# Attention backward on one core: three passes over the scores replaced by one loop of small TensorE tiles

## The chip, the cores and the metric

The kernel runs on one core of a Trainium2 chip. The metric is the device time in microseconds (us) of one execution. In the listings PE is TensorE (the matmul engine), PEld its weight loads, DVE is VectorE, ACT is ScalarE, POOL is GpSimd and SP the Sync engine, whose queue issues most DMAs (transfers). SBUF is the working memory of the core; matmuls write their results to PSUM, which VectorE and ScalarE read. The granted clock is the share of TensorE's full clock that the profile records; it stands at 1 or at 0.5 here. A tile of TensorE is a part of its 128 x 128 array: 32*128 in a listing means 32 rows and 128 columns.

## The reference

The program is the forward and the whole backward of two attention blocks, A and B, on separate inputs. Their outputs stand side by side. Block A is a linear attention and the change does not touch its arithmetic. Block B is softmax attention with 16 heads of width 28 and one shared K and V:

```python
def _B_ref(x, wq, wk, wv, wo):           # x 1x2048x448, H = 16, Dh = 28
    q = (x @ wq).reshape(B, S, H, Dh) ...                 # per head
    k = x @ wk                                            # shared by all heads
    v = x @ wv
    scores = einsum("bhqd,bkd->bhqk", q, k) * (Dh ** -0.5)
    p = softmax(scores)
    o = einsum("bhqk,bkd->bhqd", p, v)
    return o.reshape(B, S, H * Dh) @ wo
# result: out = concat(A, B) and the gradients of all eight inputs, for a given grad_out, in bf16
```

In the backward, with e = exp(scale * score) and do = grad_out_B @ wo^T, the costly products per head, query and key are these: score, dp = do.v, o = sum e*v, ds = e * (dp - D), dq = sum ds*k, dk = sum ds*q, dv = sum e*do. D is a row sum of do*o. There are 16 x 2048 x 2048 scores, which is 1024 tiles of 128 x 512. The contraction or the result of every product is only 28 wide. Both kernels pad it to 32.

## The kernel before

Block B walks over all scores three times. All matmuls use the whole array. Since a head is only 32 rows wide, four heads are put into one 128-row operand, and the other operand is block-expanded: 4 blocks of 32 rows on the diagonal and zeros elsewhere.

```python
# 1. forward: e goes to the o product and to DRAM
for g in range(4):                       # four heads each
    for qp in range(QPAIRS):             # 256 queries
        block_expand(qblk, ...)
        for t in range(NS):              # 128 keys
            st_ps = psS.tile([P, 1024], F32, name="st_ps")
            for hv in range(2):
                mm(st_ps[:, hv * 512:(hv + 1) * 512], kT_rep[:, t * P:(t + 1) * P], qblk[:, hv, :])
            e = ework.tile([P, 1024], BF16, name="e")
            nc.scalar.activation(out=e[:], in_=st_ps[:, :], func=ACT.Exp, scale=scale)
            for hv in range(2):
                mm(oaccs[hv][:, :], vaug_rep4[:, t, :], e[:, hv * 512:(hv + 1) * 512], ...)
            eng.dma_start(edram[r0:r0 + P, :], e[:, :])
# ... o, D, and don = do / rowsum, with D folded in as one more column ...
# 2. dv and dk: scores again, this time with queries on the partitions
for t in range(NS):
    for qt in range(NS):
        for g in range(4):
            mm(s_ps[:, :], qT_B[g][:, qt * P:(qt + 1) * P], kblk[:, t, :])
            nc.scalar.activation(out=e[:], in_=s_ps[:, :], func=ACT.Exp, scale=scale)
            mm(dp_ps[:, :], doT2_B[g][:, qt * P:(qt + 1) * P], vblk[:, t, :])
            nc.vector.tensor_tensor(out=ds_sb[:, :], in0=dp_ps[:, :], in1=e[:, :], op=ALU.mult)
            mm(dvT_acc[:, :], don2_B[:, qt, g * P:(g + 1) * P], e[:, :], ...)
            mm(dkT_acc[:, :], qn_B[:, qt, g * P:(g + 1) * P], ds_sb[:, :], ...)
# 3. dq: e back from DRAM, with keys on the partitions
for g in range(4):
    for qb in range(NS):
        for t in range(NS):
            # every second t: DMA of e from edram
            mm(dpt_ps[:, :], vT_rep[:, t * P:(t + 1) * P], dblk[:, qb, :])
            # dsT = dpt_ps * e on VectorE (every third by way of a ScalarE copy)
            mm(dqacc[:, :], kn_rep4[:, t, :], dsT[:, :], start=(t == 0), stop=(t == NS - 1))
# ... weight gradients, output of B ...
```

## Time and profile before

| what | value |
|---|---|
| median time, 4 runs | 2837.94 us (2831.61 to 2847.09) |
| profiled span | 2839.7 us |
| block A | 0 to 393 us |
| projections of B | 393 to 530 us |
| pass 1, forward | 530 to 1096 us (566 us, 1.10 us per exp of 1024 columns) |
| middle | 1096 to 1205 us |
| pass 2, dv and dk | 1205 to 2180 us (975 us, 0.95 us per tile) |
| pass 3, dq | 2180 to 2786 us (606 us, 0.59 us per tile) |
| tail | 54 us |

The page of the kernel before gives, in parts 1 and 4, the busy time of TensorE and the chain of work that ended last, by engine:

```profile
PE 2506.8 (88%) x11290; PEld 1063.8 (37%) x11290; DVE 1709.6 (60%) x3498; ACT 1516.5 (53%) x2431; POOL 210.7 (7%) x310
...
PE 70%; ACT 15%; DVE 7%; issue 4%; DMA 2%; POOL 1%; SPq 0%; ACTq 0%; POOLq 0%; DVEq 0%
```

An average over the span hides that each stage has its own limit. The view by stretches of the kernel before shows it. Its columns are the stretch, its length, the busy us of each engine with the number of instructions, the granted TensorE clock, the busy share of the DMA engines, and GB/s:

```profile
core 0: us, PE busy (x) PEld busy (x) DVE busy (x) ACT busy (x) POOL busy (x), PEclk, DMA share, GB/s
...
530.00:1096.00 566.00, 501.39 (x2047) 197.65 (x2047) 111.91 (x398) 500.30 (x514) 138.33 (x255) 0.99 0.65 239
1096.00:1205.00 109.00, 81.39 (x407) 39.14 (x407) 90.84 (x389) 12.22 (x23) 7.47 (x2) 0.86 0.08 26
1205.00:2180.00 975.00, 972.36 (x4348) 419.76 (x4346) 714.13 (x1072) 586.20 (x1037) 0.05 (x1) 1.00 0.01 2
2180.00:2786.00 606.00, 503.09 (x2076) 200.40 (x2077) 546.82 (x1044) 260.32 (x579) 27.65 (x4) 0.97 0.71 221
```

In the second pass TensorE is busy 972 of 975 us: that pass is bound by matmuls. In the forward pass ScalarE is busy 500 of 566 us, and it does one exp of 1023 ns after another. The costliest groups of the kernel before (part 5 of the page: line, engine, operation, tiles and shapes, count; then busy us and mean ns of one; then the idle time just before them and what ended it) say what is done twice:

```profile
L780 DVE TENSOR_TENSOR ds_sb<-dp_ps,e 128x512 bf16<-128x512 f32 x1024 | 689.2, 692 | 250.8 <-PE s_ps L96 137.2 <-PE dp_ps L96 85.5 <-ACT e L776 24.8
L776 ACT ACTIVATE e<-s_ps 128x512 bf16<-128x512 f32 x1024 | 583.6, 596 | 403.7 <-DVE ds_sb L780 292.9 <-PE s_ps L96 84.6
L650 ACT ACTIVATE e<-st_ps 128x1024 bf16<-128x1024 f32 x512 | 498.8, 1023 | 64.5 <-PE st_ps L96 62.5 <-ACT e L650 2.0
```

The exps of pass 2 (583.6 us busy) repeat those of pass 1 in the other layout. The three passes take 2256 us from 530 to 2786, with the middle part among them.

One more reading matters, since the change uses the array in several tile modes. The time line of the kernel before has a place where a 128-row matmul is followed by one of 64 rows:

```profile
441.59 0.38 PE L96 MATMUL projN_ps<-wqB_pad,xb_T_3270 128*128 128x512 bf16 x1
441.90 0.39 PE L96 MATMUL projN_ps<-wqB_pad,xb_T_3271 64*128 64x512 bf16 x1
442.22 0.23 PE L96 MATMUL ps_vn<-wvB_rep,xb_T_3268 128*128 128x128 bf16 x1
```

The starts are 0.31 and 0.32 us apart, where two 128-row matmuls of that size are 0.22 apart. A change of mode costs about 0.1 us here.

### The profile page before, as it was taken

To read this page: it belongs to the slowest core of one execution; us is meant where nothing else is said; L and a number is where in the kernel's file an instruction comes from. 1 tells how busy PE (TensorE), PEld (TensorE's weight loads), DVE (VectorE), ACT (ScalarE), POOL (GpSimd) and SP (SyncE) were. 2 spreads that over 40 slices of the span, in tenths; PEclk is the share of its full clock that TensorE was granted. 3 is DMA by queue.
4 is the path that set the end of the run, shared out by engine and by line. 5 is a ranking of instruction groups with operands and counts; after the bars stand their busy time and mean duration, and the time that the engine had idled before them with its cause. 6 is when DMAs were issued, how large, how long until landed. Compare 5 with 4: busy or idle time off the path is not lost.

```text
span 2839.7 us, 35260 instructions
## 1 busy us (share of the span) xinstructions
PE 2506.8 (88%) x11290; PEld 1063.8 (37%) x11290; DVE 1709.6 (60%) x3498; ACT 1516.5 (53%) x2431; POOL 210.7 (7%) x310
## 2 busy tenths in 40 slices
PE   4777988788888888799999999999998878888788
PEld 1334533233333333344444444444443333333333
DVE  4758402122222225777777777777776989989892
ACT  1220124888888884156666566666564444444342
POOL 1000002122222221000000000000000000000000
PEclk9887988799999999799999999999999999999999
DMA  6020210466666663000000000000001767767672
GB/s 71 1 77 4 46 59 1 156 238 241 240 239 241 238 240 116 28 1 1 1 1 1 1 1 1 1 1 1 1 1 46 239 212 233 239 207 239 206 240 71
DMA packets 266987, 296.65 MB, mean 104 GB/s; under 512 B 66464, under 2 KB 217536, under 8 KB 266800
## 3 DMA queue, kind: packets, MB, share of 16 engines
q1 hardware_dynamic: 246016, 226.82, 25.9%
q0 software_dynamic: 20784, 67.58, 6.5%
q8 instruction: 88, 1.44, 0.2%
q14 instruction: 99, 0.81, 0.1%
HBM read 144.02 MB, written 144.02 MB: 101 GB/s over the span
## 4 chain that ended last, share of the span: by engine, by line
PE 70%; ACT 15%; DVE 7%; issue 4%; DMA 2%; POOL 1%; SPq 0%; ACTq 0%; POOLq 0%; DVEq 0%
PE dkT_acc L96 10%; ACT e L650 9%; PE dp_ps L96 9%; PE dpt_ps L96 8%; PE s_ps L96 8%; PE dvT_acc L96 8%; PE dqacc L96 7%; PE st_ps L96 4%; PE tps_set L100 2%; PE gw_acc L96 1%; ACT dpt_sb L826 1%; PE ps_gx L96 1%; PE projT_ps L96 1%; PE ps_gxB L96 1%; POOL dblkT L808 1%
## 5 line engine op out<-in xcount | busy, mean ns | idle before, releaser
L780 DVE TENSOR_TENSOR ds_sb<-dp_ps,e 128x512 bf16<-128x512 f32 x1024 | 689.2, 692 | 250.8 <-PE s_ps L96 137.2
L776 ACT ACTIVATE e<-s_ps 128x512 bf16<-128x512 f32 x1024 | 583.6, 596 | 403.7 <-DVE ds_sb L780 292.9
L650 ACT ACTIVATE e<-st_ps 128x1024 bf16<-128x1024 f32 x512 | 498.8, 1023 | 64.5 <-PE st_ps L96 62.5
L96 PE MATMUL dpt_ps<-dblkT,vT_rep 128*128 128x512 bf16 x1024 | 388.9, 383 | 100.6 <-ACT dpt_sb L826 57.0
L96 PE MATMUL dkT_acc<-ds_sb,qn_B 128*128 128x512 bf16 x1024 | 385.8, 377 | 2.0 <-DVE ds_sb L780 1.8
L96 PE MATMUL dvT_acc<-e,don_B 128*128 128x512 bf16 x1024 | 385.1, 378 | 0.3 <-ACT e L776 0.3
L96 PE MATMUL dqacc<-dsT,kn_rep_3252 128*128 128x512 bf16 x1024 | 379.7, 381 | 2.1 <-DVE dsT L829 1.5
L826 ACT ACTIVATE dpt_sb<-dpt_ps 128x512 bf16<-128x512 f32 x320 | 191.1, 597 | 293.3 <-PE dpt_ps L96 291.3
L96 PE MATMUL st_ps<-qblk,kT_rep 128*128 128x512 bf16 x1024 | 305.8, 380 | 9.2 <-ACT qT_B_3247 L613 9.2
L642 DVE MEMSET qblk<- 128x512 uint32 x32 | 15.5, 485 | 462.5 <-PE st_ps L96 412.6
L96 PEld LDWEIGHTS <-vaug_rep_3250 128*128 128x128 bf16 x1024 | 99.2, 97 | 244.7 <-issue 184.4
L96 PEld LDWEIGHTS <-kn_rep_3252 128*128 128x128 bf16 x1024 | 99.8, 97 | 240.9 <-issue 157.9
L656 POOL DMA_DIRECT2D edram<-e x256 | 138.9, 542 | 484.9 <-ACT e L650 484.7
L96 PEld LDWEIGHTS <-vT_rep 128*128 128x128 bf16 x1024 | 99.7, 98 | 163.7 <-DVE dblkT L224 27.0
L96 PEld LDWEIGHTS <-don_B 128*128 128x128 bf16 x1024 | 98.5, 96 | 136.0 <-issue 43.9
L96 PEld LDWEIGHTS <-kT_rep 128*128 128x128 bf16 x1024 | 98.7, 96 | 134.1 <-issue 13.1
L96 PEld LDWEIGHTS <-qn_B 128*128 128x128 bf16 x1024 | 99.3, 97 | 122.6 <-issue 1.6
L808 POOL MEMSET dblkT<- 128x8192 bf16 x4 | 27.7, 6925 | 1421.5 <-PE dp_ps L96 989.9
L96 PE MATMUL s_ps<-kblk,qT_B_3244 128*128 128x512 bf16 x256 | 97.2, 380 | 8.0 <-DVE kblk L224 8.0
L96 PE MATMUL dp_ps<-vblk,doT_B_9380 128*128 128x512 bf16 x256 | 97.0, 379 | 0.3 <-DVE vblk L224 0.3
L96 PE MATMUL s_ps<-kblk,qT_B_3245 128*128 128x512 bf16 x256 | 97.3, 380 | 0.0
L96 PE MATMUL dp_ps<-vblk,doT_B_9381 128*128 128x512 bf16 x256 | 96.9, 379 | 0.0
(1547 smaller groups left out, 3418.4 us busy)
## 6 DMA issues: line engine op xcount, KB each, us to landing
edram<-e SPq DMA_DIRECT2D x256, 256.0 KB
edram<-e POOLq DMA_DIRECT2D x256, 256.0 KB, 2.3
xa_nat<-in_A_x_dram SPq DMA_DIRECT2D x1, 1792.0 KB
out_dram<-out_a_sb SPq DMA_DIRECT2D x16, 112.0 KB
ga_nat<-in_grad_out_dram SPq DMA_DIRECT2D x1, 1792.0 KB
out_dram<-gx_sb SPq DMA_DIRECT2D x16, 112.0 KB
xb_nat<-in_B_x_dram SPq DMA_DIRECT2D x1, 1792.0 KB
gb_nat<-in_grad_out_dram SPq DMA_DIRECT2D x1, 1792.0 KB
```

What stands on the lines that cost most here:

```text
L96: nc.tensor.matmul(out_ap, lhsT=lhsT, rhs=rhs, start=start, stop=stop, tile_position=(0, 0))
L100: nc.tensor.transpose(out_ps_ap, in_ap, ident[0:k, 0:k], tile_position=(0, 0))
L642: nc.vector.memset(qblk[:], 0.0)
L650: nc.scalar.activation(out=e[:], in_=st_ps[:, :], func=ACT.Exp, scale=scale)
L656: eng.dma_start(edram[r0:r0 + P, :], e[:, :])
L776: nc.scalar.activation(out=e[:], in_=s_ps[:, :], func=ACT.Exp, scale=scale)
L780: nc.vector.tensor_tensor(out=ds_sb[:, :], in0=dp_ps[:, :], in1=e[:, :], op=ALU.mult)
L808: nc.gpsimd.memset(dblk[:], 0.0)
L826: nc.scalar.activation(out=dpt_sb[:, :], in_=dpt_ps[:, :], func=ACT.Identity)
```

## The change

The intent is to compute each score, exp and dp once. One loop of 512 units replaces the three passes. A unit covers 2 heads, 256 keys and 256 queries. Sixty-four blocks of 8 units each cover one pair of heads and one chunk of 256 queries. A later unit does the later products, so several stages are in flight:

- Scores (unit u) and dp (unit u - 16) run on four 32-row tiles of TensorE, two each, with no block expansion.
- o and dq run on four 32-column tiles and share one PSUM bank. dv runs on four column tiles, dk on the four diagonal 32 x 32 tiles.
- dv needs e with the queries on the partitions. A DMA transposes 512 KB of e inside SBUF every two units, and e no longer goes to DRAM.
- dk needs ds in that way too. VectorE transposes ds in 32 x 32 blocks of 4-byte words (pairs of bf16).
- Of the two PSUM multiplies of a unit, VectorE does one. For the other, ScalarE copies dp to SBUF and POOL multiplies there.
- Once per block small operations finish the softmax of the block, turn do into don, form D and transpose both with TensorE.

```diff
-        QPAIRS = S // 256
-        edram = edram_pool.tile([4 * QPAIRS * NS * P, 1024], BF16, name="edram")
-        ... forward pass, middle part, dv/dk pass and dq pass, as shown above ...
+            with tc.manual_schedule():
+                for u in range(NU + 26):
+                    w = u - 16
+                    ... load qX for a chunk of queries; allocate two score and two dp buffers ...
+                    rows_SD(u, sp, dp)              # scores of u and dp of w: four row tiles in turn
+                    nc.scalar.activation(out=et[:, u % 2, 0, :], in_=sp[0][:, :], func=ACT.Exp, scale=scale)
+                    nc.vector.tensor_tensor(out=dst[:, 0, :], in0=dp[0][:, :], in1=ew[:, w % 2, 0, :], op=ALU.mult)
+                    nc.scalar.activation(out=cp[:, :], in_=dp[1][:, :], func=ACT.Copy)
+                    nc.gpsimd.tensor_tensor(out=dst[:, 1, :], in0=cp[:, :], in1=ew[:, w % 2, 1, :], op=ALU.mult)
+                    nc.scalar.activation(out=et[:, u % 2, 1, :], in_=sp[1][:, :], func=ACT.Exp, scale=scale)
+                    if u % 2 == 1:
+                        nc.sync.dma_start_transpose(en[:, :, :], et[:, :, :, :].rearrange("p a b c -> p (a b c)"))
+                    # once per block, at u = 9 (mod 8 is 1): the block's small operations
+                        nc.tensor.transpose(onp..., oTs[b]..., identF...)          # twice
+                        nc.vector.reciprocal(out=r_[:], in_=onp[:, :, :, 0:1])
+                        nc.vector.tensor_tensor(out=onv, in0=onp..., in1=r_..., op=ALU.mult)
+                        nc.vector.tensor_tensor(out=dn[:], in0=dnv, in1=r_..., op=ALU.mult)      # don
+                        nc.gpsimd.tensor_tensor(out=prod[:], in0=dnv, in1=onv, op=ALU.mult)
+                        nc.vector.tensor_reduce(out=Dq[:, :, :, 0], in_=prod[:], axis=AX.X, op=ALU.add)
+                        nc.vector.tensor_tensor(out=dn[:, :, :, 0:1], in0=Dq[:], in1=r_[:], op=ALU.mult)
+                    # once per block, at u = 13 (mod 8 is 5): transpose don into doT, with a copy
+                    x = u - 26
+                    ... dk: 8 matmuls mmt(dk_acc[32 * a:32 * a + 32, :], qX..., dsx..., (32 * a, 32 * a), ...)
+                    ... o of u - 1 and dq of u - 18: 8 matmuls on four column tiles; dv every second unit ...
+                    # last in the unit:
+                    y = u - 18
+                        nc.vector.transpose(out=dsx[b][:, tp, ...].bitcast(F32), in_=dsT[y]....bitcast(F32))
```

The rest moves: the product for do comes before the loop, the output projection of B and its reloads come after it.

## The prediction

> What bounds the kernel now. The time line of the profile splits the 2840 us span (timed median 2833.8) into stages: block A to 393 us, projections of B to 530, forward attention 530 to 1096 (566 us), a middle part to 1205, pass for dv and dk 1205 to 2180 (975 us), pass for dq 2180 to 2786 (606 us), tail of 54 us. The chain of waits is 70% TensorE, 15% ScalarE. Forward is ScalarE: 512 exps of 1024 columns, 1023 ns each, one per 1.10 us. The dv/dk pass is TensorE: four 512-column matmuls of 0.216 us start to start, 0.95 us per step, 1024 steps. The dq pass takes 0.59 us per step. So attention B is 2256 us from 530 to 2786, and the change replaces nearly all of it.
>
> What the change removes. The second set of 1024 exps (584 us busy), the second product for dp with its 512 PSUM multiplies, the store and reload of e in DRAM (128 MB each way), block-expanded operands, and the f32 transposes of o. What it adds: 256 DMA transposes of 512 KB inside SBUF, 512 DVE 32x32 transposes, 512 POOL multiplies, about 13000 small matmuls in tiles of 32 rows and/or 32 columns.
>
> Cost of one of the 512 units of the loop, from durations in the trace:
> - ScalarE: two exps and one PSUM copy of 128x512. Each lasts 596 ns, starts 0.49 us apart back to back: 1.5 us.
> - VectorE: one PSUM multiply (0.60 to 0.65 back to back), one 512-word transpose (estimate 0.6), an eighth of six small operations: 1.45 us.
> - POOL: one multiply of 128x512. The Trainium skill, GPSIMD Engine Reference, section 3.1, gives 4497 ns for 2048 columns, so an estimate of 1.15 us; no run here shows it.
> - TensorE: if four tiles run together, scores and dp 0.25 to 0.43 us, dk 0.43 to 0.5, o and dq 0.21 to 0.3, dv 0.11, plus three tile-mode changes. The trace shows what a change costs: where a 128-row matmul is followed by a 64-row one, starts are 0.31 us apart and not 0.22, so 0.1 each. With transposes 1.4 to 1.9 us. The Trainium skill, "TensorE: Matmul & The Clock Gate", Part 3, gives 3.07 times for four row tiles; this trace has no packing. Serial: above 4 us.
> - DMA: a 512 KB transpose each two units. From DRAM the trace shows 1.96 to 2.89 us of issue for one; that fits in 3.8 us.
>
> The score/dp buffers are reused after one unit, so TensorE waits for ScalarE's copy and ScalarE for the next scores: I expect 1.95 us per unit, TensorE and ScalarE both near 80% busy, hence about 1050 us of loop. Before it about 555 us (block A unchanged, dO projection moved forward, about 20 us more), after it about 140 us (reloads, o projection, all weight gradients). Sum 1745; with the risks below 1780 us.
>
> Right if: the loop has one exp pass, period 1.7 to 2.2 us, four tiles overlapping. Wrong if: the SBUF transposes issue slower than 3.8 us each (then SP is always busy and the loop about 3.4 us per unit, 2430 us in total); the diagonal dk tiles, which write one PSUM bank, do not overlap (period 2.6, 2080); POOL and DVE block each other (period 2.2 and up). If all overlaps well, period 1.65 and 1580 us.
>
> Range 1590 to 2400 us. Faster by over 2%: 0.91; within 2%: 0.02; slower: 0.07.

## The result, and the profile after

| | before | after |
|---|---|---|
| median of 4 runs | 2837.94 us | 1723.72 us (1719.94 to 1728.62) |
| ratio | 1 | 0.6078 (95% interval 0.606 to 0.6096) |
| profiled span | 2839.7 us | 1718.1 us |
| mean granted TensorE clock | 0.956 | 0.847 |

Ratios here and below are the mean time of one kernel's fast runs over that of the other's fast runs of the same rounds on the same chip, so they are not quite the ratio of the medians quoted.

The view by stretches of the changed kernel, with the columns as before:

```profile
393.00:555.50 162.50, 111.22 (x442) 38.03 (x443) 32.84 (x104) 77.59 (x121) 19.78 (x21) 0.74 0.30 67
555.50:1600.00 1044.50, 905.14 (x13568) 281.51 (x13567) 810.26 (x1476) 813.54 (x1605) 621.88 (x583) 0.84 0.82 141
1600.00:1629.00 29.00, 2.19 (x16) 1.27 (x16) 0.10 (x1) 0.21 (x1) 0.00 (x0) 0.53 0.81 172
1629.00:1718.10 89.10, 79.96 (x584) 41.42 (x584) 14.40 (x47) 24.58 (x55) 0.00 (x0) 0.94 0.17 52
```

The account closes. The loop takes about 1042 us in place of 2256. The part between block A and the loop grew from 137 to 162.5 us. After the loop come about 121 us, 29 of them a gap for reloads, in place of 54. That is -1214 + 25 + 67 = -1122 us, which is the difference of the two spans (2839.7 - 1718.1 = 1121.6).

Busy times in the loop are 87% for TensorE and 78% for ScalarE, at a clock of 0.84. No engine is full. The DMA engines are at 82%, and that is not the limit either, as two experiments show below. The costliest groups of the changed kernel (part 5 of its page):

```profile
L679 POOL TENSOR_TENSOR dsT<-cp,eT 128x512 bf16<-128x512 bf16 x512 | 590.6, 1154 | 405.6 <-ACT cp L678 345.0
L623 PE MATMUL dk_acc<-dsx,qX 32*32 32x512 bf16 x4096 | 369.9, 441 | 120.8 <-DVE dsx L780 120.8
L676 DVE TENSOR_TENSOR dsT<-dps,eT 128x512 bf16<-128x512 f32 x512 | 347.8, 679 | 165.9 <-PE dps L623 156.8
...
L780 DVE STREAM_TRANSPOSE dsx<-dsT 128x512 f32<-128x512 f32 x512 | 357.9, 699 | 1.0
```

Most of TensorE's idle time in the loop (1044.5 us less 905.1 busy) stands in one group: dk waits 120.8 us for `dsx`, the VectorE transposes of ds. How is that spread? The list of waits of the changed kernel, from 600 to 1400 us (engine, line, what it waited for: us in total, times, longest):

```profile
ACT eT L671 <- PE dps L623: 145.2, 83, 2.9
DVE dsT L676 <- PE dps L623: 124.2, 215, 1.5
PE dk_acc L623 <- DVE dsx L780: 96.8, 50, 2.2
```

Fifty waits of 1.94 us in 800 us is one in 16 us. That is once per block of 8 units. Most of the waits of ScalarE and VectorE for `dps` follow from it: nothing comes from TensorE while it stands, and in e1_early below, where it is gone, they fall to 46.4 and 57.2 us.

The start times of ScalarE's first exp in each unit give the length of every unit. I worked these out from the trace (means over blocks 8 to 59, by the place of the unit in its block):

| unit in its block | 0 | 1 | 2 | 3 | 4 | 5 | 6 | 7 | sum |
|---|---|---|---|---|---|---|---|---|---|
| us | 1.457 | 2.022 | 4.233 | 1.930 | 1.746 | 1.582 | 1.457 | 1.524 | 15.95 |

The mean over all 512 units is 1.968 us; the first blocks, which have no dk and dq yet, are shorter. The prediction had 1.95. An undisturbed unit takes 1.457 us: that is ScalarE's three operations of 128 x 512, 0.49 us apart from start to start. The mean of 1.97 is not the length of a usual unit. Unit 2 of each block takes more than twice as long. The time line of the changed kernel shows what happens there (start, length, engine, line, operation; in brackets the idle time before it and what ended it):

```profile
992.41 1.15 POOL L679 TENSOR_TENSOR dsT<-cp,eT 128x512 bf16<-128x512 bf16 x1 [0.32 <-ACT cp L678]
992.52 0.29 DVE L705 TENSOR_TENSOR onat<-sps,rl 128x128 bf16<-128x128 f32 x1
...
992.72 0.99 DVE L709 TENSOR_TENSOR don<-do_nat,rl 128x128 bf16<-128x128 bf16 x1
...
993.52 0.47 POOL L711 TENSOR_TENSOR prod<-do_nat,onat 128x128 f32<-128x128 bf16 x1
...
994.03 0.29 DVE L713 TENSOR_REDUCE Dq<-prod 128x4 f32<-128x128 f32 x1 [0.32 <-POOL prod L711]
...
994.43 0.70 DVE L780 STREAM_TRANSPOSE dsx<-dsT 128x512 f32<-128x512 f32 x1
...
995.18 1.04 PE L623 MATMUL dk_acc<-dsx,qX 32*32 32x512 bf16 x8 [1.93 <-DVE dsx L780]
```

The last transpose of a block of ds stands on VectorE behind the small operations. Of these, the product for `don` reads two operands from SBUF and takes 0.99 us: it ends at 993.71, just after POOL's multiply does (993.56). The reduction then waits for a product of POOL that stood behind the same multiply. So the transpose starts at 994.43, and dk's first matmul, the next one in TensorE's order, stands for 1.93 us. Each time the granted clock falls afterwards: from 600 to 1400 us all 50 of these waits are followed, within 4 us of their start, by a stretch of half clock of 3.4 or 6.8 us, 29% of that time in all. The Trainium skill, "TensorE: Matmul & The Clock Gate", Part 1, names an idle window of about 3.4 us for the fall to half clock, and the page's rules for kernels ask for no gaps above about 3 us. Here waits of 1.93 us, once in 16 us, went with it. The same part also tells of frequent short idles between matmul groups that make the clock swing, without saying how short. In the same stretch of other runs a fall followed 12 of 55 waits of 1.1 us (e2_lag27), 45 of 46 of about 1.75 us (e7_dve) and 36 of 45 of about 1.81 us (e8_rows). So the length alone does not decide, and what exactly the clock answers to was not isolated.

The packing of tiles works. The time line of the changed kernel, one group of scores and dp in it:

```profile
990.81 0.28 PE L623 MATMUL sps<-qT_B_3187,kT_rep 32*128 32x256 bf16 x2
990.82 0.37 PE L623 MATMUL dps<-doT,vT_rep 32*128 32x256 bf16 x2
990.93 0.28 PE L623 MATMUL sps<-qT_B_3187,kT_rep 32*128 32x256 bf16 x2
990.93 0.36 PE L623 MATMUL dps<-doT,vT_rep 32*128 32x256 bf16 x2
```

Four matmuls start within about 0.01 us, and the next four 0.11 us later, which is the time of one matmul of 256 columns.

### The profile page after: what moved, and what is told of

The parts are those of the page before. It is cut to its first block, busy times and chain, and to the rows that moved or that the text cites. A ratio compares the mean times of both kernels' runs of the same rounds, so it can differ in the third digit from the quotient of the medians.

```text
span 1718.1 us, 40732 instructions
## 1 busy us (share of the span) xinstructions
PE 1394.5 (81%) x16282; PEld 511.1 (30%) x16282; DVE 1065.9 (62%) x2113; ACT 986.5 (57%) x1907; POOL 658.5 (38%) x632
## 5 line engine op out<-in xcount | busy, mean ns | idle before, releaser
L679 POOL TENSOR_TENSOR dsT<-cp,eT 128x512 bf16<-128x512 bf16 x512 | 590.6, 1154 | 405.6 <-ACT cp L678 345.0
L623 PE MATMUL dk_acc<-dsx,qX 32*32 32x512 bf16 x4096 | 369.9, 441 | 120.8 <-DVE dsx L780 120.8
L676 DVE TENSOR_TENSOR dsT<-dps,eT 128x512 bf16<-128x512 f32 x512 | 347.8, 679 | 165.9 <-PE dps L623 156.8
L671 ACT ACTIVATE eT<-sps 128x512 bf16<-128x512 f32 x512 | 307.2, 600 | 206.7 <-PE dps L623 174.5
L780 DVE STREAM_TRANSPOSE dsx<-dsT 128x512 f32<-128x512 f32 x512 | 357.9, 699 | 1.0
L678 ACT ACTIVATE cp<-dps 128x512 bf16<-128x512 f32 x512 | 304.6, 595 | 15.8 <-PE dps L623 15.8
L681 ACT ACTIVATE eT<-sps 128x512 bf16<-128x512 f32 x512 | 310.5, 606 | 0.0
L623 PE MATMUL dps<-doT,vT_rep 32*128 32x256 bf16 x2048 | 258.9, 300 | 2.1 <-DVE dsT L676 1.5
L623 PE MATMUL oq<-eT,vaug 128*32 128x256 bf16 x2048 | 229.8, 310 | 0.0
L623 PE MATMUL oq<-dsT,kn 128*32 128x256 bf16 x2048 | 226.7, 306 | 0.0
L623 PE MATMUL sps<-qT_B_3185,kT_rep 32*128 32x256 bf16 x512 | 67.2, 314 | 11.4 <-ACT qT_B_3188 L600 9.0
L623 PE MATMUL sps<-qT_B_3186,kT_rep 32*128 32x256 bf16 x512 | 67.0, 311 | 0.7 <-ACT eT L681 0.3
L623 PE MATMUL sps<-qT_B_3187,kT_rep 32*128 32x256 bf16 x512 | 64.3, 301 | 0.5
L623 PE MATMUL sps<-qT_B_3188,kT_rep 32*128 32x256 bf16 x512 | 64.2, 301 | 0.6
```

Source lines behind the costliest of these rows:

```text
L623: nc.tensor.matmul(out, lhsT=lhsT, rhs=rhs, start=start, stop=stop, tile_position=pos, skip_group_check=True)
L671: nc.scalar.activation(out=et[:, u % 2, 0, :], in_=sp[0][:, :], func=ACT.Exp, scale=scale)
L676: nc.vector.tensor_tensor(out=dst[:, 0, :], in0=dp[0][:, :], in1=ew[:, w % 2, 0, :], op=ALU.mult)
L678: nc.scalar.activation(out=cp[:, :], in_=dp[1][:, :], func=ACT.Copy)
L679: nc.gpsimd.tensor_tensor(out=dst[:, 1, :], in0=cp[:, :], in1=ew[:, w % 2, 1, :], op=ALU.mult)
L681: nc.scalar.activation(out=et[:, u % 2, 1, :], in_=sp[1][:, :], func=ACT.Exp, scale=scale)
```

## The experiments

Three theories were on record for the 1.97 us per unit, with these letters. **A**: one stall per block, since the last transpose of ds comes after the block's small operations. **B**: the DMA transposes set the pace. **C**: small tiles count as little activity, so the half clock stays whether or not TensorE waits. The prediction's own reason, that every unit is held by the reuse of the score and dp buffers, has no letter; the units of 1.457 us in the table speak against it, and e1_early tests it too. e4_half, e6_both_half and e11_notp compute something wrong; all others agreed with the reference (how little that says of dv, see e4_half). The kernel before took 2836 to 2839 us (medians) beside them.

| run | time, us (fast runs: lowest to highest) | ratio to before, 95% | 
|---|---|---|
| changed kernel | 1723.72 (1719.94 to 1728.62) | 0.6078, 0.606 to 0.6096 |
| e1_early | 1595.12 (1592.27 to 1596.92) | 0.5619, 0.5608 to 0.5629 |
| e2_lag27 | 1616.38 (1615.15 to 1622.33) | 0.5701, 0.5688 to 0.5714 |
| e3_dkser | 1723.08 (1717.71 to 1728.45) | 0.6073, 0.6048 to 0.6098 |
| e4_half | 1724.14 (1719.28 to 1730.95) | 0.6079, 0.6061 to 0.6097 |
| e5_both | 1596.81 (1592.35 to 1605.34) | 0.5628, 0.5608 to 0.5647 |
| e6_both_half | 1587.79 (1580.38 to 1593.08) | 0.559, 0.5571 to 0.561 |
| e7_dve | 1811.82 (1808.81 to 1814.82) | 0.6381, 0.6361 to 0.6401 |
| e8_rows | 1833.57 (1826.99 to 1839.39) | 0.6446, 0.6425 to 0.6467 |
| e9_best | 1592.41 (1588.56 to 1597.26) | 0.5615, 0.5604 to 0.5626 |
| e10_pool | 1591.32 (1587.23 to 1595.62) | 0.5612, 0.5599 to 0.5625 |
| e11_notp (wrong) | 1606.76 (1598.74 to 1614.77) | 0.5661, 0.5627 to 0.5696 |
| e12_don | 1601.03 (1592.67 to 1610.04) | 0.5632, 0.5615 to 0.5649 |

### e1_early: the transpose of ds ahead of the block's small operations

```diff
+                    if 0 <= u - 18 < NU:              # now before the small operations of the block
+                        nc.vector.transpose(out=dsx[b][:, tp, ...].bitcast(F32), in_=dsT[u - 18]....bitcast(F32))
                     e = u - 9
                     if e >= 0 and e % 8 == 0 and e // 8 < NB:
...
-                    if 0 <= y < NU:                   # was last in the unit
-                        nc.vector.transpose(out=dsx[b][:, tp, ...].bitcast(F32), in_=dsT[y]....bitcast(F32))
```

> One edit to the changed kernel: in each unit the 32x32 transpose of ds is issued to VectorE before the once-per-block small operations instead of after them. Theory A (in the changed kernel the unit takes 1.46 us undisturbed, and once per block of 8 units TensorE's first dk matmul stands 1.9 us on the last transpose, which queues behind the block's small VectorE operations and their wait for POOL; the idle TensorE then also loses half its clock): the wait of dk for dsx falls from 116 us to under 30, the share of half clock in the loop from 29% to under 15%, mean unit 1.55 to 1.70 us, time 1530 to 1600 us. Theory B (the DMA transposes, busy 84% of the loop, set the pace): time within 2% of 1724, the wait moves to the dv matmuls. Theory C (small tiles count as little activity, so the half clock stays): the wait goes but the clock share stays near 0.85 and the time is 1640 to 1700 us.

Measured: 1595.12 us, 129 us less than the changed kernel. The mean unit fell from 1.968 to 1.722 us and unit 2 from 4.233 to 2.216. The list of waits of e1_early, 600 to 1400 us, in which dk no longer waits for `dsx` at all:

```profile
...
DVE dsT L676 <- PE dps L623: 57.2, 174, 2.1
ACT eT L671 <- PE dps L623: 46.4, 66, 1.8
PE dps L623 <- DVE dsT L676: 28.1, 56, 0.5
```

The same stretch by engines, first of the changed kernel, then of e1_early:

```profile
600.00:1400.00 800.00, 693.16 (x10640) 215.63 (x10640) 634.04 (x1154) 632.78 (x1255) 483.98 (x451) 0.86 0.83 143
```

```profile
600.00:1400.00 800.00, 737.44 (x12205) 255.13 (x12208) 705.75 (x1327) 723.77 (x1441) 556.73 (x520) 0.99 0.99 165
```

In the same 800 us TensorE did 12205 matmuls in place of 10640, and its clock was 0.99 in place of 0.86 (half clock in 1.5% of this stretch, no longer 29%). The only difference is where one VectorE instruction stands. Theory A holds for about half of the surplus: of the 4.29 us by which a block exceeds eight undisturbed units (15.95 - 8 x 1.457), this took away 2.06. (The mean unit, 1.722 us, ends a little above the 1.55 to 1.70 that A gave.) How much of it was the stall itself and how much the half clock after it is not separated. Theory C is out: it expected a clock near 0.85 and 1640 to 1700 us. The DMA engines went from 0.83 to 0.99 busy, so they had room. That speaks against B.

### e2_lag27: dk one unit later

```diff
-                for u in range(NU + 26):
+                for u in range(NU + 27):
-                    x = u - 26
+                    x = u - 27
```

> One edit to the changed kernel: dk of a block starts one unit later (lag 27 units, not 26), VectorE's order unchanged. Theory A: the same wait goes, by another edit, so 1530 to 1610 us and a dk wait under 30 us. Theory B: within 2% of 1724. Theory C: 1640 to 1700 us with the clock share near 0.85.

Measured: 1616.38 us. This gives the late transpose one more unit without moving it. The wait of dk for `dsx` is gone from its list, and it wins 107 us of the 129. It ends a little above the range that A gave, because the small operations still delay VectorE in unit 2 (2.83 us). The late VectorE now holds up the next `dps` matmul, 61.7 us in 800, since VectorE had not emptied a buffer. The stall moved one step on and became smaller.

### e3_dkser: dk's matmuls in the order tile by tile

```diff
-                        for m in (2 * (x % 8), 2 * (x % 8) + 1):
-                            h, B, s = m // 8, (m // 2) % 4, m % 2
-                            for a in range(4):
+                        for a in range(4):
+                            for m in (2 * (x % 8), 2 * (x % 8) + 1):
+                                h, B, s = m // 8, (m // 2) % 4, m % 2
```

> One edit to the changed kernel: the eight dk matmuls of a unit are issued tile by tile (two on one diagonal tile, then the next tile) instead of one on each of the four tiles twice; same matmuls, same result. If matmuls on different tiles run together and those on one tile one after another, a pair waits for its first and then overlaps with the next pair, so the group takes 5 x 0.213 instead of 2 x 0.213 us, about 1.1 us in place of 0.54, and the loop gains 0.3 to 0.6 us per unit: 1880 to 2020 us. If the order of tiles is without effect (all overlaps anyway, or nothing does): within 2% of 1724.

Measured: 1723.08 us, no difference. This was meant to take dk's packing away: two matmuls for the same tile in succession, then two for the next. I expected a second matmul on a busy tile to hold all those behind it. Nothing of that shows. The starts within one dk group, worked out from the trace, are at 0, 7, 14, 20 and then 230, 239, 243, 251 ns; in the changed kernel they are at 0, 4, 7, 10 and then from 230 on. The group takes 0.551 us in place of 0.541. So it seems that matmuls for other tiles start ahead of one that waits for its own tile, although they stand behind it in program order. The trace does not name the tile of a matmul; I read this from the steps of 7 ns in place of 3 or 4, as if every second one was passed over, and from the unchanged length of the group. The Trainium skill, "TensorE: Matmul & The Clock Gate", Part 3, calls matmuls "strict FIFO, no reordering" in start and end. Read so, these starts do not agree with that for starts, and the measurement decides. The experiment therefore says nothing about what dk would cost unpacked.

### e4_half: every second DMA transpose left out (dv wrong)

```diff
                         if u % 2 == 1:
-                            en = pn_.tile([P, 16, P], BF16, name="eN")
-                            nc.sync.dma_start_transpose(en[:, :, :], et...)
+                            if (u // 2) % 2 == 0:
+                                en = pn_.tile([P, 16, P], BF16, name="eN")
+                                nc.sync.dma_start_transpose(en[:, :, :], et...)
                             eN[u // 2] = en
```

> Wrong on purpose (dv, and what follows from it): only every second DMA transpose of e is issued, the dv matmuls read the last one twice. Nothing else is changed. Theory A: the DMA share in the loop halves to about 42%, time 1700 to 1730 us, the dk wait stays near 116 us. Theory B: the unit falls to 1.6 us or less and the time under 1600 us.

Measured: 1724.14 us, no difference. The stretch of e4_half, and its wait of dk:

```profile
600.00:1400.00 800.00, 692.00 (x10639) 216.68 (x10639) 634.75 (x1157) 634.79 (x1259) 486.50 (x454) 0.86 0.42 78
```

```profile
PE dk_acc L623 <- DVE dsx L782: 96.8, 50, 2.0
```

With half the DMA work (share 0.42 in place of 0.83) the stall of dk is as it was, to the tenth of a microsecond in the sum. B is out. A warning comes with it: dv used a wrong e in half of its steps, and the comparison with the reference still passed. With these inputs that comparison cannot see this error, so for dv the agreement of the other runs is weak evidence too.

### e5_both and e6_both_half: both remedies, then with half the DMA

e5_both moves the transpose early, sets dk one unit later, and issues dk ahead of the block's TensorE transposes. e6_both_half leaves out every second DMA transpose of e5_both, in the way of e4_half (dv wrong again; the comparison passed again).

```diff
+                for u in range(NU + 27):
+                    x = u - 27                        # dk, now ahead of the block's transposes
+                    ... dk as before, then the early transpose of e1_early, then the small operations ...
```

> Both earlier edits together (transpose of ds ahead of the block's small operations, and dk one unit later; dk is issued ahead of the block's TensorE transposes so that the buffer is read before it is reused). With the transpose alone moved the unit took 1.71 us, and no wait of dk was left in the list. If what remains of the excess over 1.46 us is the block's TensorE transposes and the late PSUM multiply, the extra unit brings nothing much: 1570 to 1605 us. If some wait of dk was still hidden: under 1560 us.

> The kernel with both edits, and every second DMA transpose left out (dv wrong on purpose). Theory B again, at the faster pace, where a transpose takes about 3.0 to 3.2 us of DMA time against 3.4 us for two units: if the DMA is now what limits, the time falls by more than 40 us against the run with both edits; if it is not, it stays within 1%.

Measured: 1596.81 us for e5_both, which is e1_early within its spread; the mean unit is 1.722 us in both. Once the stall is gone, more slack for dk buys nothing. Half clock is 0.2% of the stretch from 600 to 1400 us. e6_both_half took 1587.79 us, 9 us less; unit 6 of the block is the one place that changed much (1.644 to 1.457 us). In e5_both the DMA share reads 1.00, which looks like a limit; with 0.51 in its place the kernel is only 0.6% faster. A busy share of 1.00 for DMA means here that a transfer was always under way, and the loop hardly waited for it: dv waited for `eN` 7.3 us in 800.

### e7_dve: the second multiply on VectorE

```diff
-                        cp = pc_.tile([P, 512], BF16, name="cp")
-                        nc.scalar.activation(out=cp[:, :], in_=dp[1][:, :], func=ACT.Copy)
-                        nc.gpsimd.tensor_tensor(out=dst[:, 1, :], in0=cp[:, :], in1=ew[:, w % 2, 1, :], op=ALU.mult)
+                        nc.vector.tensor_tensor(out=dst[:, 1, :], in0=dp[1][:, :], in1=ew[:, w % 2, 1, :], op=ALU.mult)
```

> Undo one part of the change: the second PSUM multiply of dp goes to VectorE directly, without ScalarE's copy and POOL's multiply. VectorE then has two multiplies (about 0.62 us each back to back), the transpose (0.62) and the small operations (0.25): 2.1 us per unit against ScalarE's 1.0, so VectorE-bound, unit 2.1 to 2.4 us, time 1790 to 1950 us. If instead the copy on ScalarE was the limit of the unit, the time would fall below 1700.

Measured: 1811.82 us, 2.113 us per unit, as expected. The stretch of e7_dve:

```profile
600.00:1400.00 800.00, 666.28 (x9856) 208.36 (x9849) 758.14 (x1445) 423.29 (x794) 19.59 (x46) 0.89 0.77 133
```

VectorE is busy 758 of 800 us. The detour by ScalarE and POOL costs POOL 1154 ns for each multiply, but POOL has the time. It takes the limit off VectorE, and is worth 88 us. This run also shows something about `don` that is used at e11_notp below.

### e8_rows: scores and dp on the same two row tiles

```diff
-                            r = 64 * (1 - hp) + 32 * h
+                            r = 64 * hp + 32 * h          # dp now on the tiles of the scores
...
-                        r = 64 * (1 - hp)
+                        r = 64 * hp                       # doT is written to the same rows
```

> Packing test, correct result: dp's matmuls use the same two row tiles (of 32 rows) as the scores of their unit instead of the other two, so four tiles become two with four matmuls each. If tiles overlap and matmuls of one tile do not, scores and dp of a unit stream 4 x 107 in place of 2 x 107 ns: 0.21 us more per unit on TensorE, and as the dk stall hides part of it 40 to 120 us more in all (1765 to 1845 us). If packing were not what makes this group fast: within 1% of 1724.

Measured: 1833.57 us, the median of three fast runs; one slow run of 2001.46 us is left out. Its time line, to be held against the four lines of the changed kernel above:

```profile
1000.19 0.28 PE L623 MATMUL sps<-qT_B,kT_rep 32*128 32x256 bf16 x2
1000.31 0.27 PE L623 MATMUL dps<-doT,vT_rep 32*128 32x256 bf16 x2
1000.42 0.27 PE L623 MATMUL sps<-qT_B,kT_rep 32*128 32x256 bf16 x2
1000.53 0.27 PE L623 MATMUL dps<-doT,vT_rep 32*128 32x256 bf16 x2
```

Only two matmuls start together now, and the rounds are 0.11 us apart. The smallest time of a group of scores and dp rose from 0.326 to 0.538 us, by two rounds of 0.107. The kernel lost 110 us, that is 0.21 us for each of 512 units. (From 600 to 1400 us its half clock also rose from 29% to 37%, so the match is partly chance.) What the four tiles together are worth in this one product is shown by the starts: twice the throughput of two tiles. The group takes longer than its two rounds by about 0.1 us, which I put down to the change of tile mode after it: in the changed kernel at full clock a group of o and dq takes 0.228 us to the next start where dv follows in the same mode, and 0.334 where scores follow in another. That agrees with the Trainium skill, "TensorEngine Tiling (Array Packing)", section "Key Properties", which says that changing the mode drains TensorE; it gives no figure.

### e9_best and e10_pool: the tail

After the loop a gap of 29 us stands, and the DMA engines are 0.81 busy in it: I take it that the reloads for the weight gradients can only start when the loop's SBUF is free. e9_best (on e5_both) reorders the tail so that the output of B comes first, and keeps `wo` in SBUF. e10_pool has POOL issue the reloads in place of the Sync queue.

```diff
-            xb_nat = load_x(t4, Bx2, "xb2")                  # e9_best: moved to after the output of B
-            woB_pr = load_wo_padrows(t4, B_wo, "woB_pr2")    # e9_best: kept from before the loop
-            pn_ = ... name="ceN", bufs=11
+            pn_ = ... name="ceN", bufs=10                    # e9_best: to make room
+            nc.gpsimd.dma_start(gb_nat[:, :, :], ...)        # e10_pool: and the other reloads
```

> The kernel with both edits, and the tail reordered: after the loop of the changed kernel TensorE stands about 29 us until reloads of weights have landed (wq first). Here the padded rows of wo stay in SBUF from the start (paid for with one eN buffer fewer, 10 in place of 11), and the weights of q, k, v are reloaded after the o projection. Expected: the gap after the loop falls from 29 to about 12 us (the reload of o must still land), the loop is unchanged, 1570 to 1585 us. If the reload of o is itself late (it is last in its queue), no gain: within 0.5% of 1597.

> The kernel with both edits and the reordered tail, with the tail's reloads of x, dO and the weights issued from POOL instead of the Sync queue. In the run before, the gap after the loop was filled but the rows of the B output then waited 4.4 and 6.2 us each behind those loads' issue on the Sync queue. If that issue order was the cause, the output rows go out every 2.4 us as before and the time falls by 8 to 20 us: 1572 to 1585 us. If the DMA engines themselves are full there, it stays within 0.5% of 1592.

Measured: 1592.41 and 1591.32 us, 0.3% less than e5_both and within its spread. The chain of waits shows where the gap went. First a piece of that of e5_both (start, length, what), then one of e9_best, then of e10_pool:

```profile
1471.45 29.10 issue
```

```profile
1495.03 4.41 DMA out_dram<-out_b_sb
```

```profile
1470.60 23.27 DMA onat_B<-on_d
```

In e9_best the rows of the output wait behind the loads in one queue. In e10_pool, with the loads in another queue, the first load takes 23 us, while the others run beside it. The wait changed its name twice and the time hardly moved. I read that as the transfers of the reloads themselves being what the tail waits for; no run here took them away to prove it.

### e11_notp and e12_don: what is left per block

In e1_early a block takes 13.89 us, 2.23 us above eight undisturbed units. Units 1, 2 and 5 hold most of that (2.043, 2.216 and 2.033 us). Both runs change one thing in e5_both. e11_notp replaces the transposes of don (unit 5) with a copy of other data, so the gradients are wrong, and the comparison said so for three of them (relative errors of 127 and more). e12_don gives the product for don to POOL.

```diff
-                        tp2 = psS.tile([P, 1024], BF16, name="sps")      # e11_notp
-                        nc.tensor.transpose(tp2[...], don[b]..., identB...)        # twice
-                        nc.vector.tensor_copy(out=doT[b][r:r + 64, :], in_=tp2[r:r + 64, 0:256])
+                        nc.vector.tensor_copy(out=doT[b][r:r + 64, :], in_=qT_B[g][r:r + 64, qc * 256:(qc + 1) * 256])

-                        nc.vector.tensor_tensor(out=dn[:], in0=dnv, in1=r_..., op=ALU.mult)      # e12_don
                         nc.gpsimd.tensor_tensor(out=prod[:], in0=dnv, in1=onv, op=ALU.mult)
+                        nc.gpsimd.tensor_tensor(out=dn[:], in0=dnv, in1=r_..., op=ALU.mult)
```

> Wrong on purpose (dp of attention B, and what follows from it): the kernel with both edits, without the TensorE transposes of dO/l once per block (unit 5 of 8) and their borrowed score buffer; VectorE copies other data of the same shape. With both edits the periods of units 1, 2 and 5 are 2.03, 2.22 and 2.03 us and of the others 1.46 to 1.65. If the transposes make unit 5 long, its period falls to about 1.5 us, units 1 and 2 stay, the time falls by some 25 to 35 us unless the DMA, busy all the time there, takes it back. If unit 5 is long for another reason, its period stays at 2.0.

> One edit to the kernel with both edits: the small product dO/l (128x128, two SBUF inputs) goes from VectorE to POOL, behind POOL's own small product. On VectorE it lasted 785 ns, though the product of the same size with one PSUM input lasted 292; in the trace it ends 0.14 us after POOL's 1.15 us multiply ends, as if it waited for it. If VectorE and POOL shut each other out here and this is what delays the block's next PSUM multiply (units 1 and 2 at 2.03 and 2.22 us), unit 2 gets 0.4 to 0.8 us shorter, the mean unit falls from 1.72 to 1.62 to 1.68 us, the time to 1545 to 1582 us. If the DMA transposes, at 3.0 to 3.2 us for two units and always busy now, hold the pace, or if units 1 and 2 are long for TensorE's sake: within 1% of 1597.

e11_notp took 1606.76 us, 10 more than e5_both, where 25 to 35 less was expected. Unit 5 fell from 2.031 to 1.525 us, as expected: its surplus is the pair of transposes with their tile modes and the borrowed score buffer, together. But unit 6 rose from 1.644 to 2.196, because the stand-in was not neutral: in the time line the longer copy delays VectorE's next multiply, and the next dp matmul waits 0.36 us for that. The VectorE groups show the copy in e11_notp, then those of e5_both, with the products for `don` and `onat`, then the product for `don` in e7_dve:

```profile
L745 DVE COPY doT<-qT_B 64x256 bf16<-64x256 bf16 x57 | 61.4, 1078 | 0.9
```

```profile
L730 DVE TENSOR_TENSOR don<-do_nat,rl 128x128 bf16<-128x128 bf16 x57 | 44.7, 785 | 0.0
...
L726 DVE TENSOR_TENSOR onat<-sps,rl 128x128 bf16<-128x128 f32 x57 | 16.6, 292 | 1.9
...
L750 DVE COPY doT<-sps 64x256 bf16<-64x256 bf16 x58 | 15.6, 269 | 0.9
```

```profile
L706 DVE TENSOR_TENSOR don<-do_nat,rl 128x128 bf16<-128x128 bf16 x46 | 12.9, 281 | 0.0
```

The same copy takes 269 ns from PSUM and 1078 ns from SBUF. The product takes 292 ns with one operand in PSUM and 785 ns with both in SBUF. In both cases the slow form reads SBUF only, and POOL is at work beside it. For the product e7_dve settles the cause, though it was not made for that: there POOL's large multiply is gone, and the same product with both operands in SBUF takes 281 ns. (In the changed kernel it takes 995 on average.) For the copy no run takes POOL away. The Trainium skill, "SBUF — State Buffer", section "Who interferes with whom", states the rule: VectorE with two SBUF inputs (against a POOL instruction that reads SBUF), or in a two-port mode, shares a port pair with POOL, and one of the two fully blocks. These durations agree with it.

e12_don was to profit from that and did not: 1601.03 us, where 1545 to 1582 was expected. The product on POOL no longer meets a VectorE operation of two SBUF inputs, but the reduction on VectorE waits for POOL. From the waits of e5_both, then of e12_don:

```profile
PE sps L623 <- ACT eT L681: 29.3, 115, 0.3
PE dps L623 <- DVE dsT L676: 28.5, 57, 0.5
...
DVE Dq L734 <- POOL prod L732: 18.2, 57, 0.3
```

```profile
DVE Dq L734 <- POOL prod L731: 55.5, 57, 1.0
```

VectorE no longer has the product for don (44.7 us in 800), but it waits 37.3 us longer for POOL. What makes up units 1 and 2 is not settled by a run. The first two lines of e5_both name candidates: scores wait about twice per block for ScalarE to free a score buffer (the small operations of units 1 and 5 each borrow one), and dp waits 0.5 us once per block for VectorE's multiply, which stands behind the small operations. For unit 5 the transposes are shown.

## Why the prediction was right, and where its reason was not

- **The total.** Predicted 1780 us after an allowance for risks on a sum of 1745; measured 1723.72. The terms of the sum: before the loop 555 (measured 555.5), the loop 1050 (1042), after it 140 (121).
- **What bounds the kernel before.** The readings by stage hold: 2256 us went and 1042 came.
- **Operations from durations.** ScalarE's three operations were put at 0.49 us each from start to start, and an undisturbed unit lasts 1.457 us, which is just that. VectorE's transpose was estimated at 0.6 us and takes 0.699 on average.
- **POOL's multiply.** The estimate of 1.15 us for 512 columns came from the 4497 ns for 2048 in the Trainium skill, "GPSIMD Engine Reference", section 3.1. Measured: 1154 ns, though in bf16 and not in the page's fp32.
- **Tiles and DMA.** Four tiles overlap (e8_rows shows what happens if only two do), dk's diagonal tiles overlap in spite of one PSUM bank (four starts within 10 ns), and the DMA transposes keep up (e4_half, e6_both_half).
- **The step that failed** is this sentence: "The score/dp buffers are reused after one unit, so TensorE waits for ScalarE's copy and ScalarE for the next scores: I expect 1.95 us per unit". The number came out (1.97), the reason did not: that the mean fell so near is luck, since two things it did not name, the stall and the other once-per-block work, add up to it. Where nothing disturbs it, a unit takes 1.457 us, and TensorE's groups fit within that at full clock (0.33 at best for scores and dp, 0.54 for dk, about 0.44 on average for o, dq and dv, from start to start in the trace). About half of the surplus over that (2.06 of 4.29 us per block) went with one stall per block: the VectorE transpose that dk needs stood behind the block's small operations. This also cost TensorE its clock. Moving that one instruction made the unit 1.72 us. What is left then, 2.23 us per block, stands mostly in the units with other once-per-block work: the transposes of don are shown for unit 5, units 1 and 2 are open. In the changed kernel itself unit 5 took only 1.582 us; its surplus appears once the stall is gone.
- **The risk named for POOL and VectorE** ("block each other, period 2.2 and up") is real but small. The small product takes 0.99 us inside the chain shown at 992.72, and 0.28 us in e7_dve without POOL's multiply. It did not bind every unit.

## What to carry to other kernels

When a software pipeline runs slower than each of its engines, do not spread the surplus evenly over the steps: list the length of every step by its place in the block, and look at the longest one. An instruction on an engine that is not the bottleneck can hold back the bottleneck once per block by its mere place in program order; give the result that the bottleneck needs next the first place, and the bookkeeping the later one. A stage's busy share near 1 for DMA proves little until some of the transfers have been taken away.

## What the Trainium skill lacked or had wrong

- "TensorE: Matmul & The Clock Gate", Part 1 and its rules: the rules ask only for no gaps above about 3 us, and of shorter idles Part 1 says that they can make the clock swing, but not how short. Here waits of 1.93 us, once in 16 us, went with half clock in 29% of 600 to 1400 us; without them it was 1.5%, and the time fell from 1724 to 1595 us. Waits of 1.1 us (e2_lag27) were followed by a fall in 12 of 55 cases.
- "TensorE: Matmul & The Clock Gate", Part 3: matmuls are called strict FIFO. With dk issued tile by tile, those for free tiles seem to have started 7 to 20 ns after the first, ahead of the second one for the busy tile at 230 ns; the group took 0.551 us against 0.541.
- "TensorEngine Tiling (Array Packing)", "Key Properties": the drain at a change of mode has no figure. About 0.1 us here (0.31 from start to start in place of 0.22; 0.334 in place of 0.228 for a group of o and dq).
- "VectorE: DVE Perf Modes", "The three transpose paths": the table has only 128 x 128 in bf16 (311 ns), and no page has a duration for 4-byte words. The transpose of 128 x 512 words of 4 bytes, which carries pairs of bf16, took 699 ns on average.
- "DMA: Bandwidth & Descriptors", "Latency and other measured facts": 261 GB/s is given for the transposing DMA with a non-contiguous middle dimension. From SBUF to SBUF in the loops of the changed kernel, e1_early and e5_both 143 to 165 GB/s moved in all, with the DMA engines 83% to 100% busy.
